# One hand-written line of pieces for all engines, from the start to step 30

## The chip, the cores and the metric

The kernel runs on 1 core of one Trainium2 chip. The metric is device microseconds of that core; lower is better. Before the change: 841.99 us, median of 3 runs (841.66 to 844.39).

## The reference

Three stages in a row, all in fp32 (some weights arrive as 64-bit words and are narrowed by the kernel itself).

```python
# 1. landmark attention: q, k, v are (4, 8, 576, 64); m = 32 landmarks
q_lm = q.reshape(B, H, m, S // m, D).mean(axis=3); k_lm likewise
A  = softmax(scale * q    @ k_lm.T)      # 576 x 32
Bm = softmax(scale * q_lm @ k_lm.T)      # 32 x 32
C  = softmax(scale * q_lm @ k.T)         # 32 x 576
Z  = Bm.T / (norm1(Bm) * norminf(Bm) + 1e-6)
for _ in range(6): Z = 2 * Z - Z @ Bm @ Z
x  = A @ Z @ C @ v                       # then (B*S, H*D) = 2304 x 512
# 2. gated layer: 512 -> 1536 -> 512
x  = (sigmoid(x @ w_gate) * (x @ w_val)) @ w_out
# 3. PReLU layer: 512 -> 2048 -> 512
h  = x @ w_in; out = (relu(h) + alpha * min(h, 0)) @ w_out2
```

## The kernel before

**Stages.** For each of the four batches b the attention makes a small matrix M (`newton`, which runs the six rounds on 32x32 blocks and multiplies with C @ v) and the operand A. M is folded into the gate and value weights of each of six column blocks c (`fold`, L714, and `take`, L736), so that layer 1 is a product of the folded weights We[b, c] with A[b]. Layer 1 and layer 2 of the gated network run in 96 steps, 24 for each b: a step is one half of the tokens (288) times one tile of 128 hidden columns. `layer1` (L763 on) issues 12 matmuls into two PSUM banks (L772), then a sigmoid on ScalarE (L784 for steps before 31, L792 after), a product on VectorE (L785), and `split`, a rounded high part on ScalarE (L136) and the rest on VectorE (L137). `layer2` (L819) issues 12 matmuls two steps later, from `catch_up`. After the 96 steps the PReLU layer runs in 24 pairs (L1140 and L1184) and ends the kernel.

**Weights.** 36 tiles of 64-bit words (24 of w_gate and w_val, 12 of w_out) are loaded by SP (L679, L684) and narrowed: `narrow_scale` (ScalarE, L171), then the low bits either on ScalarE (`narrow_low`, L176) or on VectorE (`narrow_shift`, L182), then two VectorE operations (`narrow_join`, L196 and L198). `convert` does one tile whole: a gate/value tile goes to DRAM for later folds (L702) and, at the fourth tile of a block, `fold` and `take` for b = 0 follow; a w_out tile is split, with the low part on GpSimd, for tiles 1 and 3 on VectorE (`LO_DVE`). Another 32 tiles for the last layer are narrowed by `narrow_w2` or inside `layer1`: two of them at step 30, the others at the steps in `NARROW_AT`.

**First attention.** For b = 0, `first_attention` runs `att_landmarks`, then `newton`, `att_values` and `att_queries` in turns. `transposed` turns six 96-token pieces per pair of heads on TensorE (L251), copies them out on ScalarE (L256) and sums groups of 18 tokens on VectorE (L257). The weights of the softmax for C are turned on TensorE (L392) and copied by ScalarE (L393).

**Later attentions.** `later_attentions` is a generator for b = 1 to 3; each `next` is one piece. The loop over the steps takes 1.75 pieces a step for b = 0 and 2.5 for b = 1 (`ATT_PACE`).

**Order.** Nothing is ordered by hand up to step 30: each engine's order comes out of a scheduler that goes by priority in program order, with `tc.high_priority` for `newton` and some products. From step 31 (`PIN_FROM`) the step's ScalarE, VectorE and load instructions are chained by `pin`. Each engine, and each DMA queue, works its instructions off in that order: one that waits holds up all that stand behind it.

## Time and profile before

| | |
|---|---|
| median of 3 runs | 841.99 us |
| lowest, highest | 841.66, 844.39 us |
| the profiled execution | 845.21 us |
| its span, first to last instruction | 843.4 us |
| TensorE busy | 805.9 us, 96% |
| VectorE busy | 572.0 us, 68% |
| ScalarE busy | 463.7 us, 55% |
| GpSimd busy | 84.4 us, 10% |

Shares over the whole span hide the stages. Rows by stretches of time show what each engine does in a stage; the sigmoids of the steps (L784) serve as marks for where the kernel stands. A view of forms gives the mean duration of each kind of instruction; consecutive instructions of one engine overlap a little, so that such sums come out above the busy time.

### The profile page before, as it was taken

Reading aid. Unit: us, or ns where it says so; the run is one execution under the profiler, and the core shown is the slowest. Engines: PE = TensorE matmul, PEld = TensorE weight load, DVE = VectorE, ACT = ScalarE, POOL = GpSimd, SP = SyncE. Lnnn points to the kernel's source line nnn. Section 1 sums busy time; section 2 is a strip of 40 time slices with the busy share of each in tenths; the row PEclk is TensorE's granted clock in tenths of the full one; section 3 lists DMA queues with packets and bytes.
Section 4 is the critical chain, followed back from the end, with each engine's and each line's share of the span. In section 5 each row is a group of like instructions: output and inputs, shape, how many; then the busy total and the mean of one; then the engine's idle time right before and its main releaser. Section 6 shows DMA issues by size and latency. Waiting matters only on the chain.

```text
span 843.4 us, 15865 instructions
## 1 busy us (share of the span) xinstructions
PE 805.9 (96%) x6033; PEld 710.4 (84%) x6033; DVE 572.0 (68%) x1225; ACT 463.7 (55%) x978; POOL 84.4 (10%) x84
## 2 busy tenths in 40 slices
PE   4779888999999999999999999999999999999996
PEld 4458777787888878999999999898899899899895
DVE  3899988666675564667777887867645568545543
ACT  4768874466664443665555665646543446543443
POOL 0312112121110100252302000000000000000000
PEclk9659999999999999999999999999999999999999
DMA  9779966845345664878366646636633436642002
GB/s 259 274 230 279 290 214 232 230 133 153 113 103 179 227 216 137 267 250 287 129 216 233 208 147 221 217 104 206 191 112 99 144 115 202 221 158 87 1 1 75
DMA packets 75180, 150.99 MB, mean 179 GB/s; under 512 B 9296, under 2 KB 34912, under 8 KB 75104
## 3 DMA queue, kind: packets, MB, share of 16 engines
q1 hardware_dynamic: 71648, 137.40, 50.7%
q0 software_dynamic: 3456, 12.58, 4.7%
q8 instruction: 47, 0.77, 0.4%
q14 instruction: 29, 0.24, 0.1%
...
## 4 chain that ended last, share of the span: by engine, by line
PE 83%; DVE 6%; DMA 4%; issue 3%; ACT 2%; POOL 1%; SPq 1%; POOLq 0%; DVEq 0%; ACTq 0%
PE o L1184 23%; PE prod L1140 21%; PE gv L772 16%; PE acc L819 15%; PE psf L725 3%; PE psq L251 1%; DMA tq<-in_q_dram 1%; PE psc L276 1%; DMA raw<-in_moe_w_val_dram 1%; DMA w2d<-n 1%; DVE wgv L198 1%; DVE wgv L196 1%; POOL wconv L137 0%; PE psd L336 0%; DMA raw<-in_moe_w_out_dram 0%
## 5 line engine op out<-in xcount | busy, mean ns | idle before, releaser
L1140 PE MATMUL prod<-x,w 128*128 128x384 f32 x1008 | 199.7, 337 | 0.0
L1140 PEld LDWEIGHTS prod<-x,w 128*128 128x128 f32 x1008 | 180.3, 188 | 12.8 <-DVE u L1201 0.2
L772 PE MATMUL gv<-A,we 128*128 128x288 f32 x1152 | 189.1, 306 | 1.7 <-ACT g L784 1.0
L772 PEld LDWEIGHTS gv<-A,we 128*128 128x128 f32 x1152 | 163.7, 192 | 21.4 <-issue 17.7
L819 PE MATMUL acc<-gs,wconv 128*128 128x288 f32 x1152 | 180.3, 300 | 1.2 <-DVE part L1033 1.2
L1184 PE MATMUL o<-w,g2s 128*128 128x512 f32 x693 | 180.2, 393 | 0.0
L819 PEld LDWEIGHTS acc<-gs,wconv 128*128 128x128 f32 x1152 | 160.9, 189 | 11.4 <-issue 9.0
L1184 PEld LDWEIGHTS o<-w,g2s 128*128 128x128 f32 x693 | 128.4, 188 | 19.7
L1154 ACT ACTIVATE n<-h 128x384 f32<-128x384 f32 x96 | 50.4, 525 | 87.8 <-DVE h L1201 87.2
L1156 DVE SCALAR_TENSOR_TENSOR h<-n,minus_alpha,h 128x384 f32<-128x384 f32 x96 | 59.2, 617 | 56.4 <-ACT h L1155 55.7
L136 ACT CAST g2s<-h 128x384 fp32r<-128x384 f32 x77 | 39.4, 513 | 49.4 <-DVE h L1156 49.4
L1201 DVE TENSOR_TENSOR h<-u,prod 128x384 f32<-128x384 f32 x72 | 39.8, 553 | 24.3 <-PE prod L1140 20.6
L796 ACT CAST gs<-g 128x288 fp32r<-128x288 f32 x65 | 28.2, 433 | 44.9 <-DVE g L795 44.7
L137 DVE TENSOR_TENSOR g2s<-h,g2s 128x384 fp32r<-128x384 f32 x77 | 42.8, 556 | 13.9 <-ACT g2s L136 11.9
L1155 ACT ACTIVATE h<-h 128x384 f32<-128x384 f32 x96 | 50.4, 525 | 2.7
L795 DVE TENSOR_TENSOR g<-g,gv 128x288 f32<-128x288 f32 x65 | 29.3, 450 | 29.4 <-PE gv L772 25.7
L798 DVE TENSOR_TENSOR gs<-g,gs 128x288 fp32r<-128x288 f32 x65 | 29.7, 457 | 25.9 <-ACT gs L796 25.6
L1184 PE MATMUL o<-w,g2r 128*128 128x512 f32 x171 | 45.2, 393 | 0.0
L171 ACT ACTIVATE raw<-raw 128x512 f32<-128x512 f32 x62 | 40.8, 670 | 8.0 <-DMA raw<-in_moe_w_val_dram 4.0
L792 ACT ACTIVATE g<-gv 128x288 f32<-128x288 f32 x65 | 26.6, 410 | 31.8 <-PE gv L772 31.5
L257 DVE TENSOR_REDUCE lm<-psq 128x32 f32<-128x288 f32 x64 | 27.8, 454 | 17.2 <-ACT kT L256 10.1
L1184 PEld LDWEIGHTS o<-w,g2r 128*128 128x128 f32 x171 | 31.7, 188 | 5.1
...
## 6 DMA issues: line engine op xcount, KB each, us to landing
w<-w7d SPq DMA_DIRECT2D x48, 512.0 KB, 3.4
raw<-in_moe_w_out_dram SPq DMA_DIRECT2D x28, 512.0 KB, 5.2
wgv<-wgvd POOLq DMA_DIRECT2D x24, 512.0 KB, 5.4
w7d<-w SPq DMA_DIRECT2D x24, 512.0 KB, 3.1
raw<-in_moe_w_in_dram SPq DMA_DIRECT2D x16, 512.0 KB, 4.7
...
wgvd<-wgv SPq DMA_DIRECT2D x12, 512.0 KB, 5.1
...
```

The source lines that it names most:

```text
L136: nc.scalar.copy(dst[:, 0, :], src)
L137: (nc.gpsimd if lo == "pool" else nc.vector).tensor_tensor(out=dst[:, 1, :], in0=src, in1=f32(dst[:, 0, :]), op=ALU.subtract)
L171: return nc.scalar.activation(w[:, :, 1], w[:, :, 1], AF.Copy, scale=2.0 ** -112)
L772: nc.tensor.matmul(ps[:, :HB], lhsT=We[b, c, j][:, a, 256 * i + P * s : 256 * i + P * s + P], rhs=att[b, j, "A"][half][:, e, :], start=(n ...
L798: nc.vector.tensor_tensor(out=gs[:, 1, :], in0=g, in1=f32(gs[:, 0, :]), op=ALU.subtract)
L819: nc.tensor.matmul(acc[m][:, :HB], lhsT=wout_sb[f][:, a, P * m : P * m + P], rhs=gs[:, e, :], start=(f == f0 and n == 0), stop=(f == f1 - ...
L1140: nc.tensor.matmul(ps[:, :HG], lhsT=w[:, a, kk], rhs=x7[i, op, kk][:, e], start=(n == 0), stop=(n == 5),)
L1154: nc.scalar.activation(n, h, AF.Relu, scale=-1.0)
L1155: nc.scalar.activation(h, h, AF.Relu)
L1156: nc.vector.scalar_tensor_tensor(out=h, in0=n, scalar=minus_alpha[:, f : f + 1], in1=h, op0=ALU.mult, op1=ALU.add)
L1184: nc.tensor.matmul(acc, lhsT=gs[:, a, P * t : P * t + P], rhs=w2_out[f][:, e, :], start=(count[i, u] == 1 and k == 0), stop=(count[i, u] = ...
L1201: nc.vector.tensor_tensor(out=c, in0=x, in1=ps, op=ALU.add)
```

## The change

The order of TensorE, VectorE, ScalarE, GpSimd and SP up to step 30 is written out as a string of 549 letters, `LINE`, each one piece of work, in a block in which the scheduler keeps the order as written. What was one piece is cut where it passes from one engine to another: `convert` becomes S (ScalarE's part), J (VectorE's) and P (store, or split); `layer1` up to step 30 becomes X (matmuls), Y (sigmoid), y (product), Z (high part), z (low part), and C is `catch_up`; f and t, F and T are the high and low parts of the folds for b = 0 and b = 1. k, q, K, Q, l, L, a, A, v, V and n are the pieces of the first attention, b the pieces of the later ones, p a load of tokens, r a load of a raw weight tile, R a reload of stored weights, s a sigmoid ahead of time to load its table, and h 12 transposes of no use other than to keep TensorE going.

For b = 0 the tokens are loaded in another order, 18 consecutive tokens of one landmark on one partition, so that the landmark sums are additions along a partition (24 VectorE additions in place of 16 reductions), the transposes are 128x128 (36 in place of 48), and the turn of the softmax for C is one VectorE transpose. The rows of the output for b = 0 are stored in that order, in more and smaller transfers. Off VectorE go: the shift for the six even w_out tiles (to ScalarE), the low parts of w_out tiles 1 and 3 (to GpSimd), small scalings and the copies of M for b = 0, and the scaling of C @ v (to ScalarE). Onto VectorE go the low part of A for one half of the heads of b = 0 (from GpSimd), one copy, and the turn just named.

By the end of the line 79 pieces of the later attentions are taken, of 40 for b = 1 and b = 2 each, 39 for b = 3 and two times 8 for the Newton rounds; the rest follows at 4.5 pieces a step from step 31. The two tiles that `narrow_w2` made at step 30 move to steps 33 and 54.

```diff
-    ATT_FROM, ATT_PACE, NEWTON_AHEAD, LO_DVE = 1, (1.75, 2.5), 2000, (1, 3)
+    ATT_FROM, ATT_PACE, NEWTON_AHEAD, LO_DVE = 1, (1.75, 4.5), 2000, ()
...
+    FIRST_DVE, FIRST_POOL = ('q11',), ('0',)
...
+    LINE_NEEDS = {
+        ("l", 0): (("k", 2), ("q", 2)), ("L", 0): (("K", 2), ("Q", 2)),
+        ("L", 1): (("l", 2),),
+        ("a", 0): (("q", 5), ("l", 1)), ("A", 0): (("Q", 5), ("L", 1)),
+        ("v", 0): (("k", 5), ("l", 1)), ("V", 0): (("K", 5), ("L", 1)),
...
+    LINE = (
+        "kkpkqqKrkqkqKKKlqSlavlQQLSpaJrQLLKaSSQvSrLvVlJrSPaaSPJnhVnhVSPJnJJPJrJnvSQPbSnbJ"
+        "nvvnaSJnRSAnpJJSvrnPSvnArSnAbbVPnpvrraPnJSAraAPAPrPVbVbnJASVrAsPPbnbVJSVSJnbhAaf"
+        "SAhStJrPaXRJpYPPyPbXSZPprzYfbyXtYyJbbZXJrzZJPCrJrSbbYCyzrJrPZbXYSyXSJzPZbzfpYySt"
+        "CPpJCXJYSyJfXbZCStpbZzpPYbbrCyZbbXSzbbYPrJbPrpyPbSCbpzZzbSJrbbXpYbySbCPXZbbJCJYp"
+        "PybzZfbtbPXYyrbZzbCXYzCSyZbXJSrYbypPCzbPXYryZbzPSJPCbXYJrSJZPzfpCtyZbzPXYyZbXYby"
+        "zXbbYCpyZzbbrCJbXYZbbrPzyCpbFTZXYyzZzbCbrXYyFRZXYCbTpybbCRzbprXYyFZCZTzXYyzbZXzp"
+        "YyrXYbbryCZbpzFXYTCbZyzbXYybrbpCbZbrXRrzYybbRCZzpXYybbCFTCbCZzZbzCbFT"
+    )
...
-    NARROW_AT = {*range(34, 53, 2), *(58 + 29 * i // 20 for i in range(20))}
+    NARROW_AT = {33, *range(34, 55, 2), *(58 + 29 * i // 20 for i in range(20))}
...
+    def load_first(src, j, nm):
+
+        flat = src[0, 4 * j : 4 * j + 4].rearrange("h (p r) d -> (h p) r d", r=R0)
+        parts = []
+        for r0, r1 in ((0, CUT0), (CUT0, R0)):
+            t = ws_tile(nm, (P, r1 - r0, D), F32)
+            nc.sync.dma_start(out=t, in_=flat[:, r0:r1])
+            parts.append(t)
...
+        (x, y), w = parts, first[j, "work"]
+        add(w[:, :5], x[:, :5], x[:, 5:])
+        yield
+        add(w[:, 5:], y[:, :4], y[:, 4:])
+        add(w[:, :4], w[:, :4], w[:, 5:])
+        add(w[:, :2], w[:, :2], w[:, 2:4])
+        add(w[:, :1], w[:, :1], w[:, 4:5])
+        add(
+            sums[:, a], w[:, 0:1].to_broadcast([P, 2, D]), w[:, 1:2].to_broadcast([P, 2, D])
+        )
...
+        for i in range(3):
+            r = 2 * (3 * n + i)
+            c = r >= CUT0
+            t, r = parts[c], r - CUT0 * c
+            nc.tensor.transpose(
+                ps[:, P * i : P * i + P], t[:, r : r + 2].rearrange("p r d -> p (r d)"), ident
+            )
+        to = first[j, nm][n // 2][:, 3 * (n % 2) : 3 * (n % 2) + 3]
+        (nc.vector.tensor_copy if dve else nc.scalar.copy)(
+            to.rearrange("p i c -> p (i c)"), ps[:, : 3 * P]
+        )
+        if n == 2:
+            del pre[nm, j]
...
+        if b == 0:
+            et = apool.tile([P, R0, LM], F32, tag="et", name="et", bufs=1)
+            nc.vector.transpose(out=et.rearrange("p r l -> p (r l)"), in_=e)
+            att[b, j, "et"] = et
+            return
...
-        nc.vector.tensor_scalar(out=cv, in0=ps[:, :D], scalar1=rd, scalar2=None, op0=ALU.mult)
+        nc.scalar.activation(cv, ps[:, :D], AF.Copy, scale=rd)
...
-            split(a2, at, lo="pool" if b == 0 else "dve")
+            nc.scalar.copy(a2[:, 0], at)
+            yield
+            (nc.gpsimd if b == 0 and str(j) in FIRST_POOL else nc.vector).tensor_tensor(
+                out=a2[:, 1], in0=at, in1=f32(a2[:, 0]), op=ALU.subtract
+            )
...
-                nc.vector.tensor_copy(
+                (nc.scalar.copy if bs[0] == 0 else nc.vector.tensor_copy)(
...
+    def first_loads():
+
+        for j in range(2):
+            for nm, src in (("k", k), ("q", q)):
+                pre[nm, j] = load_first(src, j, "t" + nm)
+        raw_ahead(2)
+        for j in range(2):
+            pre["v", j] = load_first(v, j, "tv")
+        raw_ahead(RAW0 - 2)
...
+    def tile_scale():
+
         kind, c, pr = conv.popleft()
         raw = raws.pop((kind, c, pr))
+        narrow_scale(raw)
         if kind == "o":
+            if c % 2:
+                to = words(raw)[0][:, :, 0]
+            else:
+                to = apool.tile([P, NW], F32, tag="n2", name="n2", bufs=1)
+                narrow_low(raw, to)
+        else:
+            j, u = divmod(pr, 2)
+            if u == 0:
+                wgv[c, j] = ws_tile("wgv", dtype=F32)
+            to = wgv[c, j][:, u]
+            narrow_low(raw, to)
+        scaled.append((kind, c, pr, raw, to))
+
+    def tile_join():
+
+        kind, c, pr, raw, to = scaled.popleft()
+        shifted = kind == "o" and c % 2 == 1
+        if shifted:
+            narrow_shift(raw)
+        narrow_join(raw, to, shifted)
+        joined.append((kind, c, pr, to))
+
+    def tile_done():
+
+        kind, c, pr, to = joined.popleft()
+        if kind == "o":
+            wout_sb[c] = ws_tile("wconv")
+            split(wout_sb[c], to, lo="dve" if c in LO_DVE else "pool")
             return
         j, u = divmod(pr, 2)
         if u == 1:
+            nc.sync.dma_start(out=wgvd[c, j], in_=wgv[c, j])
...
+    def product_one():
+        products.append(step_one(next(begun)))
+    def sigmoid_one():
+        *which, pss = products.popleft()
+        g = bpool.tile([P, HB], F32, tag="g", name="g", bufs=G_BUFS)
+        nc.scalar.activation(g, pss[0][:, :HB], AF.Sigmoid)
+        sigmoids.append((*which, g, pss[1]))
+    def gate_one():
+        *which, g, ps = sigmoids.popleft()
+        nc.vector.tensor_tensor(out=g, in0=g, in1=ps[:, :HB], op=ALU.mult)
+        gates.append((*which, g))
+    def high_one():
+        *which, g = gates.popleft()
+        gs = bpool.tile([P, 2, HB], F32R, tag="gs", name="gs", bufs=GS_BUFS)
+        nc.scalar.copy(gs[:, 0], g)
+        highs.append((*which, g, gs))
+    def low_one():
+        *which, g, gs = highs.popleft()
+        nc.vector.tensor_tensor(out=gs[:, 1], in0=g, in1=f32(gs[:, 0]), op=ALU.subtract)
+        behind.append((*which, gs))
...
+    def keep_busy():
+        ps = bank("idle", "acc")
+        for i in range(12):
+            nc.tensor.transpose(ps[:, P * (i % 4) : P * (i % 4) + P], ident, ident)
...
+    whole = {
+        "X": product_one, "Y": sigmoid_one, "y": gate_one, "Z": high_one, "z": low_one, "C": catch_up, "S": tile_scale,
+        "J": tile_join, "P": tile_done, "r": lambda: raw_ahead(1), "p": load_ahead,
+        "f": lambda: fold_high(0, folded), "t": lambda: fold_low(folded),
+        "F": lambda: fold_high(1, folded_next), "T": lambda: fold_low(folded_next), "h": keep_busy, "b": attend, "s": preload, "R": reload_one, "W": narrow_w2,
+    }
+    done = dict.fromkeys((*streams, *whole), 0)
+    E = mybir.EngineType
+    with tc.manual_schedule(engines={E.PE, E.DVE, E.Activation, E.Pool, E.SP}):
+        for n in LINE:
+            for other, least in LINE_NEEDS.get((n, done[n]), ()):
+                assert done[other] >= least, (n, done[n], other)
+            for other, lead in LINE_LEADS.get(n, ()):
+                assert done[other] >= done[n] + lead, (n, done[n], other)
+            if n in whole:
+                whole[n]()
+            else:
+                next(streams[n], None)
+            done[n] += 1
+    in_line[0] = False
+    for at in range(PIN_FROM, len(steps)):
...
-            if at == NARROW_FROM:
-                with tc.high_priority(NARROW_AHEAD):
-                    narrow_w2()
-                    narrow_w2()
...
-            r, p = divmod(rem, TP)
-            step = min(P - done, TP - p)
+            rr = R if bb else R0
+            half_, rem = divmod(rem, HB)
+            r, p = divmod(rem, S // rr)
+            step = min(P - done, S // rr - p)
             nc.sync.dma_start(
-                out=outv[bb, SIDE[r], p : p + step, :], in_=ob[done : done + step, :]
+                out=outv[rr][bb, 2 * r + half_, p : p + step, :], in_=ob[done : done + step, :]
```

## Rows read from the trace of the kernel before

**Rows 1.** By stage: length; busy PE, PEld, DVE, ACT, POOL; clock, DMA share, GB/s.

```profile
0.00:50.70 50.70, 29.76 (x385) 18.84 (x385) 34.58 (x100) 26.70 (x63) 8.59 (x12) 0.78 0.79 249
50.70:100.90 50.20, 48.37 (x410) 40.90 (x411) 47.48 (x110) 45.26 (x97) 10.31 (x8) 0.91 0.90 285
100.90:142.90 42.00, 35.19 (x386) 28.96 (x385) 36.64 (x95) 27.17 (x60) 9.92 (x10) 0.96 0.69 211
142.90:212.00 69.10, 68.64 (x706) 54.71 (x704) 44.38 (x116) 39.05 (x86) 10.76 (x16) 1.00 0.61 184
212.00:265.00 53.00, 52.25 (x732) 45.38 (x731) 36.53 (x112) 30.75 (x75) 5.80 (x6) 1.00 0.44 129
265.00:460.00 195.00, 195.00 (x1555) 182.97 (x1554) 127.49 (x238) 103.17 (x223) 39.00 (x33) 1.00 0.64 212
```

**Rows 2.** ScalarE in order of time: the sigmoids of steps 0, 10 and 30.

```profile
54.71 0.41 ACT L784 ACTIVATE g<-gv 128x288 f32<-128x288 f32 x1
...
100.88 0.45 ACT L784 ACTIVATE g<-gv 128x288 f32<-128x288 f32 x1
...
211.91 0.41 ACT L784 ACTIVATE g<-gv 128x288 f32<-128x288 f32 x1 [0.42 <-PE gv L772]
```

**Rows 3.** Chain that ended last: one step's layer 1 and layer 2.

```profile
267.31 1.60 PE gv L772 x12
268.91 1.59 PE acc L819 x12
```

**Rows 4.** TensorE's forms from 180 to 260 us, busy us and mean ns.

```profile
L772 PE MATMUL gv<-A,we 128*128 128x288 f32 x177 | 32.1, 311 | 0.0
...
L725 PE MATMUL psf<-wgv,m 64*32 64x512 f32 x48 | 4.7, 601 | 0.0
...
L408 PE MATMUL psv<-vt,et 96*32 96x64 f32 x192 | 4.0, 222 | 0.0
```

**Rows 5.** VectorE's 58 forms up to 212 us: first, last, and those touched.

```profile
L257 DVE TENSOR_REDUCE lm<-psq 128x32 f32<-128x288 f32 x50 | 21.8, 453 | 13.4 <-ACT kT L256 9.1 <-ACT qT L256 4.0
...
L196 DVE TENSOR_SCALAR raw<-raw 128x512 uint16<-128x512 uint16 x13 | 9.7, 759 | 0.1
...
L196 DVE TENSOR_SCALAR wgv<-raw 128x512 uint16<-128x512 uint16 x18 | 9.6, 557 | 0.0
...
L182 DVE TENSOR_SCALAR raw<-raw 128x512 uint32<-128x512 uint32 x13 | 5.4, 429 | 0.0
...
L137 DVE TENSOR_TENSOR wconv<-raw,wconv 128x512 fp32r<-128x512 f32 x2 | 2.5, 1243 | 0.0
...
L990 DVE TENSOR_SCALAR minus_alpha<-alphaT 128x16 f32<-128x16 f32 x1 | 0.2, 174 | 0.0
```

**Rows 6.** ScalarE's 27 forms up to 212 us: first, a table load, last.

```profile
L171 ACT ACTIVATE raw<-raw 128x512 f32<-128x512 f32 x32 | 20.8, 671 | 8.0 <-DMA raw<-in_moe_w_val_dram 4.0 <-DMA raw<-in_moe_w_out_dram 4.0
...
L784 ACT ACT_TABLE_LOAD x6 | 7.7, 1283 | 1.1 <-PE gv L772 1.0
...
L319 ACT ACTIVATION_READ_ACCUMULATOR bm<-psb,bmx 128x1 f32 x2 | 0.4, 193 | 0.0
```

**Rows 7.** GpSimd and VectorE at the same moment, in order of time.

```profile
30.21 1.16 POOL L441 TENSOR_TENSOR ta<-ta,am 128x576 f32<-128x576 f32 x1 [28.90 <-DVE nr L551]
30.23 1.16 DVE L552 TENSOR_SCALAR nr<-nr 128x2 f32<-128x2 f32 x1
```

**Rows 8.** GpSimd's costliest form up to 212 us.

```profile
L137 POOL TENSOR_TENSOR wconv<-raw,wconv 128x512 fp32r<-128x512 f32 x10 | 13.6, 1371 | 62.4 <-ACT wconv L136 55.4 <-DVE we L137 6.9
```

**Rows 9.** ScalarE in order of time: a wait for a weight tile.

```profile
18.38 0.65 ACT L171 ACTIVATE raw<-raw 128x512 f32<-128x512 f32 x1 [3.39 <-DMA raw<-in_moe_w_val_dram]
```

**Rows 10.** DMA from 0 to 60 us, 40 slices of 1.5 us; two issues' sizes.

```profile
GB/s 0 87 312 263 256 261 253 261 260 262 258 371 388 384 403 412 384 397 374 401 410 169 8 0 49 311 342 207 3 0 82 289 344 279 335 277 134 93 284 410
...
raw<-in_moe_w_out_dram SPq DMA_DIRECT2D x6, 512.0 KB, 6.4
...
tk<-in_k_dram SPq DMA_DIRECT2D x4, 288.0 KB, 5.3
```

More of the change, by code (lines that the diff above doesn't have):

```diff
@@ L1 @@
 from collections import deque
+from itertools import count
 from contextlib import ExitStack, nullcontext
@@ L263, in transposed, with first_sums, add @@
         return x
+    def first_sums(nm, j):
+        a, parts = "qk".index(nm), pre[nm, j]
+        if (j, "sums") not in first:
+            first[j, "sums"] = ws_tile("sums", (P, 2, 2, D), F32)
+            first[j, "work"] = ws_tile("work", (P, 9, D), F32)
+            first[j, "lm"] = ws_tile("lm", (P, 2, 4, LM), F32)
+        sums = first[j, "sums"]
+        def add(out, x, y):
+            nc.vector.tensor_tensor(out=out, in0=x, in1=y, op=ALU.add)
+        (x, y), w = parts, first[j, "work"]
[8 more added lines that the diff above has]
+        )
@@ new lines, in first_landmarks, with first_scores @@
+    def first_landmarks(j, ps_tile):
+        sums, lm = first[j, "sums"], first[j, "lm"]
+        ps = ps_tile("psd")[:, : 8 * LM]
+        for a in range(2):
+            nc.tensor.transpose(
+                ps[:, P * a : P * a + P], sums[:, a].rearrange("p e d -> p (e d)"), ident
+            )
+        nc.scalar.copy(lm.rearrange("p a h l -> p (a h l)"), ps)
+    def first_scores(j, ps_tile):
+        ps = ps_tile("psb")[:, :LM]
+        landmark_products(ps, j, first[j, "lm"])
+        landmark_scores(0, j, ps)
@@ new lines, in parts_of, with first_products @@
+    def parts_of(b, j):
+        return att[b, j, "T"] if b else (first.get((j, "q")), first.get((j, "k")), first[j, "lm"])
+    def first_products(pss, heads, lm, xs):
+        for turn_ in range(2):
+            for i, (u, hh, h) in enumerate(heads):
+                e, g = (i + turn_) % 2, 2 * u + hh
+                d = slice(D * e, D * e + D)
+                for x, i0, n in zip(xs, (0, 6), (6, 3)):
+                    nc.tensor.matmul(
+                        pss[e][LM * h : LM * h + LM, LM * i0 : LM * (i0 + n)].rearrange(
+                            "p (i c) -> p i c", i=n
+                        ),
+                        lhsT=lm[d, g],
+                        rhs=x[d, :, LM * g : LM * g + LM],
+                        start=True,
+                        stop=True,
+                    )
@@ L738, in take @@
             We[b, c, j] = ws_tile("we")
[L739 removed]
+            last = split(We[b, c, j], pss[j])
+        return last
     def store_folded(c, pss):
@@ L1044, in tile_landmark_attention_glu_prelu, with step_one @@
         order = [(h, f, f0, f1) for h, f0, f1 in segs for f in range(f0, f1)]
-        for i, (half, f, f0, f1) in enumerate(order):
-            at = 24 * b + i
-            behind.append((b, half, f, f0, f1, layer1(at, b, half, f)))
+        steps.extend((b, *o) for o in order)
+    def step_one(at):
+        b, half, f, f0, f1 = steps[at]
+        return b, half, f, f0, f1, layer1(at, b, half, f)
+    products, sigmoids, gates, highs = deque(), deque(), deque(), deque()
+    folded, folded_next = deque(), deque()
```

373 lines of the change are left out of this document (249 added, 124 removed), and 1 row of the table LINE_NEEDS.

## The prediction

> **What bounds the kernel now.** I read the table by stage first [rows 1], then the sigmoids as marks [rows 2]. From 212 us on TensorE is busy nearly all the time (52.3 of 53.0 us, then 195.0 of 195.0), so work that is moved past that point costs what it takes on TensorE, and the change can only gain before it. There the reader is to see three stages. Up to 50.7 us no engine is full: TensorE 29.8, VectorE 34.6, ScalarE 26.7 us, clock granted at 0.78. From 50.7 to 100.9 us, steps 0 to 10, VectorE is full (47.5 of 50.2) and ScalarE nearly (45.3). From 100.9 to 212 us, steps 10 to 30, TensorE looks busy (35.2 of 42.0, then 68.6 of 69.1).
>
> That last figure hides waits. One step costs TensorE 1.60 + 1.59 = 3.2 us [rows 3]. From 180 to 260 us I see 177 layer-1 matmuls, so 14.75 steps (47 us), three folds (4.7 us) and four attention groups (192 matmuls at 48 a group) [rows 4]; I estimate 4 us for the Newton rounds among them, which leaves (80 - 47 - 4.7 - 4) / 4 = 6.1 us a group. By these prices the work between the sigmoids of steps 10 and 30 is 20 x 3.2 = 64, seven folds at 1.6 = 11, some 2.75 groups = 17 and one Newton run 3: 95 us. It took 211.91 - 100.88 = 111 us. About 16 us are lost there, to waits for VectorE and for loads.
>
> **Positions instead of pieces.** Every engine's order changes at once, so no edit has a price by itself. I add up what each engine must do up to the same mark, take the fullest one, and compare the marks. For the sums each letter of the line got the mean durations of its instructions [rows 5, 6]; instructions overlap, since the 58 forms of VectorE up to 212 us add up to 183 us where the stages show 163 busy [rows 1], so sums count 0.89 for VectorE and, in the same way, 0.91 for ScalarE.
>
> **What VectorE loses and gains.** Off: the shift of six w_out tiles and their in-place join, 6 x (429 + 759 - 557) ns = 3.8 us; two low parts of 1.243 us, 2.5 us [rows 5]; two narrowed tiles, 3.1; scalings and copies, 2.9; and 0.45 of an attention group with the beginnings of a fifth, 5.7, which are only postponed. On: the turn for C, 1.5; a low part and a copy, 1.3; and the landmark sums. These were 16 reductions at 453 ns, 7.3 us [rows 5]. The 24 additions have no row; by VectorE's small and large operations they lie between 5 and 11 us, and I take 8.5. Net 14 us of rows, 12 busy: 163 becomes about 151 (149 to 154). Adding up the letters gives 154, of which 49 before the first X, 49 from there to the eleventh, 55 to the end. ScalarE comes to about 143, against 138: 46, 50 and 47. TensorE has 47 us in the second part (ten steps, five folds, 1.45 groups) and 88 in the third (20 steps 64, seven folds 11, 1.65 groups 10, Newton 3). GpSimd stays near 30. The 48 idle transposes and the turns of b = 0 stand ahead of the first X, where TensorE has 24 us of work in 60: covered. The small scalings that ScalarE takes over have no row; I took the 193 ns of its last form [rows 6] for ten of them, 2 us (1 to 4), in its sum.
>
> ScalarE's figure holds the unseen term. A table load takes 1.283 us [rows 6], and the scores of the later groups stand between sigmoids; I count eight loads in the second part, 10 us, estimated from the order of the letters. The bounds are 4 loads and 16: 5 us less, 10 more.
>
> **Where the Trainium skill speaks against it.** GpSimd's operation at 30.21 us takes 1.16 us, and a VectorE operation on 128x2 elements beside it takes the same 1.16 us [rows 7], where the last form of the VectorE view, on 128x16, takes 174 ns [rows 5]. The Trainium skill, "SBUF - State Buffer", section "Who interferes with whom", says that these two engines share one pair of ports under an exclusive lock; the row agrees. By that rule the two low parts moved to GpSimd (1.371 us each [rows 8]) could hold VectorE up for as long as they take and return nothing of the 2.5 us above. The Trainium skill, "ScalarE: Activation LUTs", section "Rules for kernel authors", wants all functions of one table set done before a switch and sets 2.7 us for it; the row of 1.283 us decides here, and by the page the second part would be 11 us longer on ScalarE.
>
> **The first sigmoid.** Before, ScalarE stood 3.39 us at a weight tile queued ahead of the landmarks [rows 9], while loads ran at about 260 GB/s for tokens and 390 for weights, with slices of nothing where SP waited [rows 10]. After the change the fifth S is the 40th letter; it needs 3.5 MB of tokens and five weight tiles of 512 KB: 13.6 + 6.7 us and 2.4 to start, so 23 us, and is done at 24.4. From there to the first X ScalarE has 36.9 us of rows, 33.6 busy, and a table load: 59.3. VectorE, from the first tokens at 5.5 us, has 49: 54.5 at the earliest. So the first sigmoid falls at about 61.5 us, and not at 54.7 [rows 2]: the change narrows 17 tiles ahead of it where the old order had narrowed six or so. This costs 7 us and is the price for a lighter second part. Should ScalarE not wait for tiles, it could be 58; should both engines wait for each other as before, 66.
>
> **The later marks.** The second part is even: 49 VectorE, 50 ScalarE, 47 TensorE, and 15 MB of transfers that fit (at 300 GB/s, 50 us at worst, and weights ran at 390). SP issues them in the order of the line: a token load whose buffer is not free holds up the weight tiles behind it and so S, and a store of narrowed weights waits for J. At the 94% that VectorE reached there before [rows 1] it takes 53: step 10 at 114.7 us, 14 behind the old 100.9. In the third part VectorE has 55 and ScalarE 47 beside TensorE's 88; TensorE is the bound, as it was from 180 to 260 us with the same load, and the price per group already holds the waits of that stretch. Step 30 comes at 202.7 us against 211.9. From the 9.2 us, the postponed 0.55 group goes off, 0.55 x 6.1 = 3.3. It is done from step 31 to 43, where VectorE is at 69% [rows 1]: TensorE's price is all of it. The two postponed tiles cost VectorE 2 us there and nobody else. The more numerous output stores for b = 0 are issued on SP amid the last layer, where TensorE has work enough; if not covered they would be a few transfers of under half a us. The gain is 5.9 us. The profiled execution, 845.2 us with a span of 843.4, becomes 839; it lies 0.4% above the median, and against the median of 841.99 the time becomes 836.
>
> **Rivals.** *A denser line* (gain 10 to 16 us). The second part runs full from 58 us: step 10 at 108, step 30 at 196, minus 3.3: 12.6 gained, 829; with waits of 180 to 260 us gone too, some 4 more, 825. For it: in a fixed order nothing unwanted can come ahead, as the tile did [rows 9]. Against it: three engines would have to be full at once.
> *No change worth measuring* (840 to 844): less than 2.5 us, 0.3%, is about what a measurement of this kernel can tell from nothing. It comes about if the line does not what it says, that is if the second part keeps its waits and only trades steps against tiles.
> *Slower, by waits in the second part.* The place is the stretch between the first and the eleventh X, where all three engines carry about 50 us and each piece of ScalarE or VectorE holds the next of the other up, with the order fixed: a late piece cannot be passed by. At a fill of 75% it takes 67 us, step 10 comes at 128 and step 30 at 216; with 3.3 for the rest, 7.6 us lost: 850. It decides at a fill of 85%: step 10 at 120.6 leaves nothing. VectorE had 95% in one stage and 87% in the next [rows 1], which is for the forecast, but it was then the one full engine, which is for this.
>
> **How the numbers follow.** Forecast, gain 3 to 11 us (831 to 839): 0.48, and its time is 836. Denser, 825 to 831: 0.16. No change: 0.15. Slower: 0.21. The first two are faster: 0.64; same 0.15; slower 0.21. The range for eight in ten runs from 821 (the denser case, with five table loads fewer) to 848, short of the full price of the slow case.
>
> **What would show it.** Right: the first sigmoid near 61 us, the eleventh near 115, the 31st near 203; VectorE's busy time up to there near 151; TensorE without gaps after the eleventh; a granted clock of 1.00 from the first X (the 0.91 of the old second stage [rows 1] would cost 9% of 47 us, some 4). Wrong: an eleventh sigmoid after 121, more than twelve table loads between the first and the eleventh, SP or GpSimd standing at a load while weights are wanted, or a stage past step 31 that is longer by more than 4 us.

## The result, and the profile after

The changed kernel takes 835.03 us (median of 4 runs, 834.33 to 835.8) beside 841.83 for the kernel before: a ratio of 0.9913, 95% interval 0.989 to 0.9935. A second set beside the last experiments gave 836.3 and 842.97, ratio 0.9929 (0.9907 to 0.9951). So it is 6.8 us faster (6.7 in the second set), against a forecast of 5.9 and a time of 836. The profiled executions are further apart, 845.21 and 834.3 us, since that of before lies 3.4 us above its median. Marks are compared below, and differences of one us between marks of two kernels are not read: up to step 10 the same order gave marks up to 1.5 us apart from run to run.

| sigmoid of step | 0 | 10 | 30 | 31 | 45 | end of span |
|---|---|---|---|---|---|---|
| before, us | 54.7 | 100.9 | 211.9 | 217.0 | 282.2 | 843.4 |
| forecast | 61.5 | 114.7 | 202.7 | | | |
| after | 61.1 | 107.6 | 185.2 | 199.9 | 270.5 | 832.6 |

Between the marks, before and after: 46.2 and 46.5 (steps 0 to 10), 111.0 and 77.6 (10 to 30), 5.1 and 14.7 (30 to 31), 65.2 and 70.6 (31 to 45), 561.2 and 562.1 (the rest). The gain of 33.4 us is all in the third part; 6.4 us are lost ahead of the first sigmoid, and 16 are given back right behind step 30.

ScalarE after, in order of time, the sigmoids that [rows 2] shows of before:

```profile
61.09 0.43 ACT L1342 ACTIVATE g<-gv 128x288 f32<-128x288 f32 x1
...
107.63 0.41 ACT L1342 ACTIVATE g<-gv 128x288 f32<-128x288 f32 x1
...
185.15 0.41 ACT L1342 ACTIVATE g<-gv 128x288 f32<-128x288 f32 x1 [0.58 <-DVE gs L1358]
```

By stage, columns as in [rows 1], cut at the marks; first after, then before from step 10 on:

```profile
0.00:61.10 61.10, 42.60 (x703) 34.93 (x703) 48.91 (x131) 44.62 (x102) 14.55 (x19) 0.75 0.96 331
61.10:107.60 46.50, 45.08 (x476) 37.74 (x478) 42.67 (x106) 39.59 (x88) 9.72 (x7) 1.00 0.81 260
107.60:185.20 77.60, 77.32 (x824) 67.60 (x813) 53.72 (x139) 40.73 (x99) 12.90 (x15) 1.00 0.50 154
185.20:199.90 14.70, 13.86 (x139) 10.66 (x137) 8.65 (x22) 7.81 (x16) 2.20 (x3) 1.00 0.62 189
199.90:270.50 70.60, 68.64 (x905) 59.52 (x905) 48.37 (x138) 47.03 (x107) 8.47 (x10) 1.00 0.48 146
```

```profile
100.90:211.90 111.00, 103.74 (x1087) 83.58 (x1086) 80.92 (x210) 66.12 (x144) 20.68 (x25) 0.98 0.64 194
...
217.00:282.20 65.20, 64.45 (x827) 56.70 (x826) 41.67 (x121) 35.49 (x83) 6.86 (x8) 1.00 0.44 133
```

Two things are to be seen. After the first sigmoid TensorE has no more gap worth naming (45.1 of 46.5, then 77.3 of 77.6), so from 61 us on the kernel is as long as TensorE's work. And the third part got shorter by more than its gaps: before, TensorE was busy for 103.7 us there and idle for 7. The rest is work that now lies elsewhere, and work that takes less time. TensorE's forms in the third part, before and then after:

```profile
L819 PE MATMUL acc<-gs,wconv 128*128 128x288 f32 x240 | 42.5, 311 | 1.2 <-DVE part L1033 1.2
L772 PE MATMUL gv<-A,we 128*128 128x288 f32 x238 | 42.2, 310 | 0.0
L725 PE MATMUL psf<-wgv,m 64*32 64x512 f32 x128 | 11.3, 601 | 0.0
```

```profile
L1061 PE MATMUL gv<-A,we 128*128 128x288 f32 x238 | 36.1, 301 | 0.0
L1104 PE MATMUL acc<-gs,wconv 128*128 128x288 f32 x192 | 29.5, 303 | 0.0
L1015 PE MATMUL psf<-wgv,m 64*32 64x512 f32 x96 | 7.1, 601 | 0.0
```

Layer 1 has the same 238 matmuls in both and keeps TensorE busy for 6.1 us less (why is not shown: the mean of one is 301 ns beside 310). Layer 2 has 48 matmuls fewer, so four steps, and the folds 32 fewer, so two. TensorE's sequence right behind step 30 shows where the layer-2 steps went:

```profile
185.95 1.83 PE L1104 MATMUL acc<-gs,wconv 128*128 128x288 f32 x12
187.72 1.09 PE L1015 MATMUL psf<-wgv,m 64*32 64x512 f32 x16
...
195.09 1.09 PE L1015 MATMUL psf<-wgv,m 64*32 64x512 f32 x16
196.11 1.84 PE L1061 MATMUL gv<-A,we 128*128 128x288 f32 x12
```

Four layer-2 steps and two folds come before the next layer 1, that of step 31 at 196.11. The line's last letters are the work that had been left over.

### The profile page after: what moved, and what is told of

It reads as the page before. It is cut to its first block, busy times and chain, and to the rows that moved or that the text cites. A ratio compares the mean times of both kernels' runs of the same rounds, so it can differ in the third digit from the quotient of the medians.

```text
span 832.6 us, 16450 instructions
## 1 busy us (share of the span) xinstructions
PE 802.2 (96%) x6313; PEld 715.7 (86%) x6313; DVE 567.2 (68%) x1213; ACT 467.4 (56%) x994; POOL 85.3 (10%) x85
## 4 chain that ended last, share of the span: by engine, by line
PE 89%; DMA 5%; DVE 3%; ACT 1%; issue 1%; SPq 1%; POOL 0%; DVEq 0%; ACTq 0%; POOLq 0%
PE o L1541 24%; PE prod L1497 21%; PE gv L1061 18%; PE acc L1104 18%; PE psf L1015 3%; DMA raw<-in_moe_w_val_dram 2%; PE psq L313 1%; DMA raw<-in_moe_w_out_dram 1%; DMA rawA<-in_moe_w_val_dram 1%; PE psc L424 1%; PE psz L726 1%; PE psd L496 0%; SPq L296 0%; PE psa L424 0%; PE psv L592 0%
## 5 line engine op out<-in xcount | busy, mean ns | idle before, releaser
L1497 PE MATMUL prod<-x,w 128*128 128x384 f32 x1008 | 199.9, 337 | 0.6 <-ACT p L1565 0.6
L1061 PE MATMUL gv<-A,we 128*128 128x288 f32 x1152 | 177.6, 300 | 1.3 <-ACT g L1077 0.8
L1061 PEld LDWEIGHTS gv<-A,we 128*128 128x128 f32 x1152 | 157.9, 188 | 21.5 <-issue 16.1
L1104 PE MATMUL acc<-gs,wconv 128*128 128x288 f32 x1152 | 175.0, 299 | 0.0
L1104 PEld LDWEIGHTS acc<-gs,wconv 128*128 128x128 f32 x1152 | 158.6, 188 | 6.6 <-issue 5.7
L1513 DVE SCALAR_TENSOR_TENSOR h<-n,minus_alpha,h 128x384 f32<-128x384 f32 x96 | 59.2, 617 | 54.4 <-ACT h L1512 53.7
L1558 DVE TENSOR_TENSOR h<-u,prod 128x384 f32<-128x384 f32 x72 | 39.8, 553 | 24.4 <-PE prod L1497 20.7
L1558 DVE TENSOR_TENSOR h<-p,prod 128x384 f32<-128x384 f32 x24 | 13.3, 553 | 27.4 <-PE prod L1497 27.4
```

Source lines behind the costliest of these rows:

```text
L1061: nc.tensor.matmul(ps[:, :HB], lhsT=We[b, c, j][:, a, 256 * i + P * s : 256 * i + P * s + P], rhs=att[b, j, "A"][half][:, e, :], start=(n ...
L1104: nc.tensor.matmul(acc[m][:, :HB], lhsT=wout_sb[f][:, a, P * m : P * m + P], rhs=gs[:, e, :], start=(f == f0 and n == 0), stop=(f == f1 - ...
L1497: nc.tensor.matmul(ps[:, :HG], lhsT=w[:, a, kk], rhs=x7[i, op, kk][:, e], start=(n == 0), stop=(n == 5),)
L1513: nc.vector.scalar_tensor_tensor(out=h, in0=n, scalar=minus_alpha[:, f : f + 1], in1=h, op0=ALU.mult, op1=ALU.add)
L1558: nc.vector.tensor_tensor(out=c, in0=x, in1=ps, op=ALU.add)
```

## The experiments

**The same pieces in the scheduler's order.**

```diff
-    with tc.manual_schedule(engines={E.PE, E.DVE, E.Activation, E.Pool, E.SP}):
+    with nullcontext():
```

> The changed kernel with the same pieces in the same program order, but without the block that keeps the order: the scheduler orders every engine. Theory A, the fixed order gains (TensorE without gaps between the sigmoids of steps 10 and 30, 78 us): without it that stretch goes back to 95 us or more and the kernel to 845 to 860 us. Rival B, less VectorE work and the new token layout gain, whatever the order: 833 to 838 us, the stretch at 78 to 84 us.

872.04 us, ratio 1.0352 (1.0315 to 1.0388): 30 us slower than the kernel before, and worse than the theory that the order is what counts had put it. The first sigmoid comes at 72.7, steps 10 to 30 take 92 us. The pieces without the written order are a loss.

**The edits in the old order.** The kernel before with the low parts of w_out tiles 1 and 3 on GpSimd, the low bits of the even tiles on ScalarE and the scaling of C @ v on ScalarE:

```diff
-    ATT_FROM, ATT_PACE, NEWTON_AHEAD, LO_DVE = 1, (1.75, 2.5), 2000, (1, 3)
+    ATT_FROM, ATT_PACE, NEWTON_AHEAD, LO_DVE = 1, (1.75, 2.5), 2000, ()
...
-        nc.vector.tensor_scalar(out=cv, in0=ps[:, :D], scalar1=rd, scalar2=None, op0=ALU.mult)
+        nc.scalar.activation(cv, ps[:, :D], AF.Copy, scale=rd)
...
-            to = words(raw)[0][:, :, 0]
-            narrow(raw, to)
+            if c % 2:
+                to = words(raw)[0][:, :, 0]
+                narrow(raw, to)
+            else:
+                to = apool.tile([P, NW], F32, tag="n2", name="n2", bufs=1)
+                narrow(raw, to, act=True)
```

> The kernel before with three of the edits alone: the low parts of w_out tiles 1 and 3 on GpSimd, the low bits of the six even w_out tiles on ScalarE, the scaling of C @ v on ScalarE; some 8 us less VectorE work in rows before step 30. Rival B: 835 to 838 us, most of the gain. Theory A: 839 to 843 us, since VectorE is full only from 50 to 100 us and TensorE's order stays.

848.39 us, ratio 1.0076 (1.005 to 1.0102). One theory expected most of the gain, the other about the old time, and both miss: with less VectorE work the kernel became 6.8 us slower. Steps 0 to 10 take 49.1 us (46.2 before), steps 10 to 30 112.6. The next run answers for 2.3 us of this; the rest stays open.

**Of these, the two low parts alone.**

```diff
-    ATT_FROM, ATT_PACE, NEWTON_AHEAD, LO_DVE = 1, (1.75, 2.5), 2000, (1, 3)
+    ATT_FROM, ATT_PACE, NEWTON_AHEAD, LO_DVE = 1, (1.75, 2.5), 2000, ()
```

> The kernel before with one of the three edits that came out slower together (848.4 against 841.8): only the low parts of the w_out tiles 1 and 3 go to GpSimd, the order is the scheduler's. Theory A (GpSimd needs longer for a low part and the gv of those steps waits for it, or its subtraction holds VectorE up): 843 to 847, and steps 0 to 10 take over 47 us. Theory B (the loss is that of the narrowing on ScalarE and of the scalings there): within 1 us of 841.8, steps 0 to 10 in 46 us.

845.44 us, ratio 1.0027 (1.0016 to 1.0038); 2.3 us slower. Steps 0 to 10 take 50.2 us, 4.0 more; steps 10 to 30 take 107.1, 3.9 less, but beside an execution of before that lies 3.4 us above its median, so the marks do not settle where the 2.3 us are lost. What the move does to VectorE stands in the order of time, GpSimd's two low parts and the VectorE instructions beside them:

```profile
52.86 2.91 POOL L137 TENSOR_TENSOR wconv<-raw,wconv 128x512 fp32r<-128x512 f32 x2 [6.93 <-ACT wconv L136]
```

```profile
53.30 1.48 DVE L196 TENSOR_SCALAR raw<-raw 128x512 uint16<-128x512 uint16 x1
54.57 1.51 DVE L196 TENSOR_SCALAR wgv<-raw 128x512 uint16<-128x512 uint16 x1
```

These two forms have means of 759 and 557 ns in [rows 5]; beside GpSimd they took 1480 and 1510. VectorE's narrowing forms up to 212 us, this kernel first, then the changed one:

```profile
L196 DVE TENSOR_SCALAR raw<-raw 128x512 uint16<-128x512 uint16 x13 | 12.8, 1015 | 0.7 <-ACT raw L171 0.7
L196 DVE TENSOR_SCALAR wgv<-raw 128x512 uint16<-128x512 uint16 x18 | 10.7, 619 | 0.0
```

```profile
L233 DVE TENSOR_SCALAR wgv<-raw 128x512 uint16<-128x512 uint16 x18 | 8.3, 459 | 0.0
L233 DVE TENSOR_SCALAR raw<-raw 128x512 uint16<-128x512 uint16 x6 | 4.6, 759 | 0.4
```

In the old order the two forms cost (1015 - 759) x 13 + (619 - 557) x 18 = 4.4 us more than before, and six tiles of a third form 1.0 us less: 3.4 us, against 2.5 of subtractions taken off (over all narrowing forms VectorE has 61.5 us instead of 55.5). In the line the two forms run at 459 and 759 ns, not above those of before. That this stretching is what made the kernel slower fits, and is not shown by itself.

**The same undone in the changed kernel**, the two low parts back on VectorE:

```diff
-    ATT_FROM, ATT_PACE, NEWTON_AHEAD, LO_DVE = 1, (1.75, 4.5), 2000, ()
+    ATT_FROM, ATT_PACE, NEWTON_AHEAD, LO_DVE = 1, (1.75, 4.5), 2000, (1, 3)
```

> The changed kernel with one edit undone: the low parts of the w_out tiles 1 and 3 are subtracted on VectorE again, not on GpSimd. Theory A (VectorE's work ahead of step 30 is what sets the marks, and a moved instruction returns its length): two subtractions of about 1.2 us come back on VectorE in the stretch to the eleventh sigmoid, of which VectorE is full, so the time is 1 to 2.5 us above the changed kernel's 835.0, that is 836 to 837.5. Theory B (the GpSimd subtraction holds VectorE up for as long as it saved, or the two fall into idle time): within 0.8 us of it.

837.43 us, ratio 0.9938 (0.9925 to 0.995), 1.1 and 2.4 us above the two medians of the changed kernel. The first sigmoid is at 63.5, where seven runs of the same order up to it (the changed kernel twice, and five that differ later or by the idle transposes alone) have 61.1 to 62.6. The later mark speaks for a small return by the move. By the times alone the two kernels are not told apart, since the intervals overlap.

**By hand up to step 10 only.** The first 311 letters, up to just ahead of the eleventh X, keep their order; the rest of the line is given in the same order, but to the scheduler.

```diff
-        for n in LINE:
+        for n in LINE[:311]:
...
+    with nullcontext():
+        for n in LINE[311:]:
```

> The changed kernel with the order kept by hand only up to the eleventh sigmoid (the first 311 letters); the other 238 pieces are given in the same order, but to the scheduler, which orders the engines. Theory A (the 33 us that the third part gained come from the order inside it): the eleventh sigmoid stays at 107.6 within 1.5, steps 10 to 30 take 90 to 95 us instead of 77.5 (92 with the whole line given to the scheduler), and the time is 847 to 853. Theory B (they come from the state in which the line leaves the kernel at step 10: tiles narrowed, tokens there, attention of the next group done): steps 10 to 30 take 77 to 81, and the time is 834 to 839.

850.41 us, ratio 1.009 (1.0076 to 1.0104); steps 10 to 30 take 91.7 us. So 14 us of the third part's gain come from the order inside it; the other 19 are there without it. But TensorE was busy there from end to end. The fold matmuls of this kernel from 107.6 to 185.2 us:

```profile
L1015 PE MATMUL psf<-wgv,m 64*32 64x512 f32 x96 | 16.8, 601 | 0.0
```

The same six folds keep TensorE for 16.8 us instead of the 7.1 shown with the result. In order of time, one fold in this kernel, and below it one in the changed kernel:

```profile
112.82 1.05 PE L1015 MATMUL psf<-wgv,m 64*32 64x512 f32 x4
113.80 0.30 PE L592 MATMUL psv<-tv,et 96*32 96x64 f32 x2
114.03 1.04 PE L1015 MATMUL psf<-wgv,m 64*32 64x512 f32 x2
```

```profile
107.95 1.61 PE L1015 MATMUL psf<-wgv,m 64*32 64x512 f32 x16
```

Two matmuls of a fold take as long as four (1.04 and 1.05 us), and sixteen in one piece 1.61: they run side by side while nothing of another shape stands between them. The Trainium skill, "TensorEngine Tiling (Array Packing)", section "Key Properties", says that tiles work in parallel and that a change of the tiling drains the engine; the rows agree in that each block begins anew at over 1 us. The kernel before ties the matmuls of a fold for b = 0 to one VectorE instruction (`behind_of`, L733), so that they become ready together; the changed kernel has no such tie. So this run, and the first one, lack the tie as well as the order; the pieces in the scheduler's order with the tie were not run, but the next run has the folds in one piece. In the first one the fold matmuls up to 460 us took 10 of the 30 us more than in the kernel before, which stands first:

```profile
L725 PE MATMUL psf<-wgv,m 64*32 64x512 f32 x384 | 31.6, 620 | 0.5 <-DVE m L594 0.2 <-DVE wgv L198 0.2
```

```profile
L1015 PE MATMUL psf<-wgv,m 64*32 64x512 f32 x384 | 41.9, 611 | 3.6 <-DMA wgv<-wgvd 3.6
```

**TensorE alone by hand, from step 10 on.** As the run before, with TensorE's order restored:

```diff
-    with nullcontext():
+    with tc.manual_schedule(engines={E.PE}):
         for n in LINE[311:]:
```

> As the run that kept all engines by hand only up to the eleventh sigmoid, but with TensorE alone kept by hand in the rest of the line too (VectorE, ScalarE, GpSimd and the DMA queue are ordered by the scheduler there). In that run the third part took 91.7 us, TensorE busy throughout, with the same 96 fold matmuls at 16.8 us busy instead of 7.1: the scheduler had put other small matmuls between them. Theory A (what the order is worth in the third part is TensorE's own sequence, above all folds in one piece): steps 10 to 30 take 77 to 81 us, the fold matmuls 7 to 8 us, and the time is 834 to 839. Theory B (the other engines' sequence matters as much, because their pieces hold each other up): 85 to 91 us, and the time is 843 to 850.

845.18 us, ratio 1.0028 (1.0016 to 1.004); steps 10 to 30 take 87.4 us. The folds are in one piece again (8.0 us for the 96), yet only 4.3 of the 14 us come back. TensorE's two longest waits from 108.8 to 196.2 us (the changed kernel has none over 0.3 us from 107.6 to 185.2):

```profile
PE pse L560 <- ACT e L531: 2.9, 1, 2.9
PE psf L1015 <- ACT e L531: 1.2, 1, 1.2
```

With TensorE's sequence fixed and ScalarE's not, an exponential that ScalarE has put off holds up everything behind it, folds included (5.4 us idle). TensorE is also busy for longer, 82.0 us instead of 77.3; 1.9 of that is one layer-2 step more ahead of the mark (204 matmuls for 192). The theory that TensorE's sequence is what counts (77 to 81 us) falls; the other one (85 to 91) holds.

**TensorE alone by hand, whole line.**

```diff
-    with tc.manual_schedule(engines={E.PE, E.DVE, E.Activation, E.Pool, E.SP}):
+    with tc.manual_schedule(engines={E.PE}):
```

> The changed kernel with TensorE alone kept by hand in the whole line; the other engines and the DMA queue are ordered by the scheduler. With everything given to the scheduler it took 872 us, with the first sigmoid at 72.7, steps 0 to 10 in 53.4 and steps 10 to 30 in 92. Theory A (TensorE's sequence is what counts from the first sigmoid on, the other engines' and the queue's order before it): the first sigmoid at 68 to 74, steps 0 to 10 in 46 to 50, steps 10 to 30 in 77 to 82, the time 842 to 852. Theory B (where VectorE and ScalarE are full, their order counts too): steps 0 to 10 take 53 us or more, the time 852 to 870.

862.29 us, ratio 1.0252 (1.021 to 1.0295): the first sigmoid at 74.7, steps 0 to 10 in 53.5, steps 10 to 30 in 87.2. The marks are those of the profiled execution, which is the slowest of four (868.16). Again the second theory: before step 10, too, a fixed TensorE gains nothing while VectorE and ScalarE are ordered otherwise.

**Fewer tiles ahead of the first X.** The prediction put the later first sigmoid down to the tiles narrowed ahead of it. Here the letters S, J, P and r past the eighth tile move behind the first X, which becomes the 139th letter instead of the 170th (the J that ends the line's first row goes as well):

```diff
...
-        "nvvnaSJnRSAnpJJSvrnPSvnArSnAbbVPnpvrraPnJSAraAPAPrPVbVbnJASVrAsPPbnbVJSVSJnbhAaf"
-        "SAhStJrPaXRJpYPPyPbXSZPprzYfbyXtYyJbbZXJrzZJPCrJrSbbYCyzrJrPZbXYSyXSJzPZbzfpYySt"
+        "nvvnanRAnpvrnPvnArnAbbVPnpvraPnAaAAVbVbnAVAsbnbVVnbhAafAhtaXJSJpSYJJSySSbrXJSZrPp"
+        "PrzPYJfSbryPXPtJYSySJbSbSZJXrPRzJZPPPCSPrJJbrbJYPCryJzrSrJrZPbXYSyXSJzPZbzfpYySt"
...
```

> The changed kernel with the line's narrowing beyond the eighth tile moved from ahead of the first X to behind it, the rest in the same order. If narrowing 17 tiles first is what makes the first sigmoid late, it comes at 48 to 54 us instead of 61.1. If VectorE and ScalarE set the eleventh sigmoid all the same, that stays at 105 to 110 us and the kernel at 834 to 837 us; if the first X is what counts, the kernel goes to 826 to 829 us.

851.87 us, ratio 1.0122 (1.0085 to 1.0158). The first sigmoid comes at 61.5, and the sixth at 97.6 instead of 80.6; the eleventh comes at 124.7, which neither theory had. Stages from 50 us on, the changed kernel first, then this one:

```profile
50.00:61.50 11.50, 10.89 (x132) 8.53 (x138) 7.58 (x15) 8.69 (x22) 3.77 (x4) 0.73 0.82 309
61.50:80.60 19.10, 18.88 (x218) 14.95 (x203) 18.06 (x45) 16.39 (x37) 4.46 (x3) 1.00 0.91 291
```

```profile
50.00:61.50 11.50, 10.42 (x120) 8.11 (x121) 3.58 (x7) 5.64 (x15) 1.40 (x1) 0.70 0.17 63
61.50:80.60 19.10, 13.63 (x110) 10.28 (x108) 17.18 (x37) 13.96 (x28) 5.03 (x5) 0.82 0.60 200
```

VectorE now has 3.6 us of work in the 11.5 us ahead of the first sigmoid, and loads run at 63 GB/s. The tiles had filled time in which the way to the first sigmoid left VectorE free, and behind it they come late: TensorE, in its fixed order, is busy for 13.6 of the next 19.1 us instead of 18.9. In the changed kernel the chain of waits to the first sigmoid passes over the load of a weight tile, then over C @ v, M and the first fold:

```profile
34.01 7.27 DMA rawA<-in_moe_w_val_dram
...
51.21 1.48 PE psv L579 x48
...
56.80 1.07 PE psf L1015 x16
```

In this run the same stretch of it, from C @ v on, is held up by something else: TensorE has no work from 48.07 us until a token load of the next batch lands, 11.9 us after its issue.

```profile
50.45 0.69 PE L307 MATMUL psq<-ident,tq 96*128 96x96 f32 x6 [2.39 <-DMA tq<-in_q_dram]
```

So the run shows that narrowing fewer tiles first does not bring the sigmoid to 48 to 54 us; the 2.4 us of this wait may hide a smaller gain.

**Without the idle transposes.** The letter h is left out of the line.

```diff
-        "kkpkqqKrkqkqKKKlqSlavlQQLSpaJrQLLKaSSQvSrLvVlJrSPaaSPJnhVnhVSPJnJJPJrJnvSQPbSnbJ"
+        "kkpkqqKrkqkqKKKlqSlavlQQLSpaJrQLLKaSSQvSrLvVlJrSPaaSPJnVnVSPJnJJPJrJnvSQPbSnbJ"
-        "nvvnaSJnRSAnpJJSvrnPSvnArSnAbbVPnpvrraPnJSAraAPAPrPVbVbnJASVrAsPPbnbVJSVSJnbhAaf"
+        "nvvnaSJnRSAnpJJSvrnPSvnArSnAbbVPnpvrraPnJSAraAPAPrPVbVbnJASVrAsPPbnbVJSVSJnbAaf"
-        "SAhStJrPaXRJpYPPyPbXSZPprzYfbyXtYyJbbZXJrzZJPCrJrSbbYCyzrJrPZbXYSyXSJzPZbzfpYySt"
+        "SAStJrPaXRJpYPPyPbXSZPprzYfbyXtYyJbbZXJrzZJPCrJrSbbYCyzrJrPZbXYSyXSJzPZbzfpYySt"
```

> The changed kernel without the 48 transposes of no use. If they keep the clock up: the granted clock in the first 59 us falls under 0.74 and the steps after it are slower, 836 to 839 us. If they only stand in TensorE's way (one dozen lies on the chain at 54.7 us, 2.1 us): first sigmoid at 59 instead of 61.1, 833 to 834 us.

836.57 us, ratio 0.9927 (0.9902 to 0.9952): not told apart from the changed kernel, and the first sigmoid at 61.7 and steps 0 to 10 in 46.5 us meet neither theory. The granted clock is 0.53 instead of 0.67 from 20 to 40 us, 0.67 instead of 0.50 from 40 to 50, and 1.00 from the first sigmoid on in both: the idle transposes shift the slow stretch, and no mark shows anything else.

**Less left for later.** Nine more attention pieces at the line's end:

```diff
-        "YyrXYbbryCZbpzFXYTCbZyzbXYybrbpCbZbrXRrzYybbRCZzpXYybbCFTCbCZzZbzCbFT"
+        "YyrXYbbryCZbpzFXYTCbZyzbXYybrbpCbZbrXRrzYybbRCZzpXYybbCFTCbCZzZbzCbFTbbbbbbbbb"
```

> The changed kernel with nine more attention pieces at the end of the line, so that less attention work is left for the stretch after step 31. Theory A (work that is postponed costs its TensorE time wherever it stands, since TensorE has no gap from the eleventh sigmoid on): the sigmoid of step 30 stays, that of step 31 comes 4 to 6 us later, that of step 45 stays within 1 us of 270.5, and the time is within 1 us of 835.0. Theory B (postponed work costs more than its TensorE time, because behind step 31 VectorE and ScalarE have the steps' own work and the next group's scalings in front of it): step 45 comes 2 to 4 us earlier, and the time is 831 to 833.

833.86 us, ratio 0.9897 (0.9882 to 0.9912): the lowest time of all, 1.2 and 2.4 us below the two medians of the changed kernel, with intervals that overlap: faster than it by the medians, not beyond doubt. The sigmoid of step 31 did not come 4 to 6 us later but 1.4, the one of step 40 5.7 later, that of step 45 at 269.6; the stretch from 31 to 45 takes 68.3 us instead of 70.6 (70.8 in the second set). That lies between the two theories.

**TensorE in program order after step 31 as well.** As the run before, and:

```diff
     for at in range(PIN_FROM, len(steps)):
+        with tc.manual_schedule(engines={E.PE}) if at < 44 else nullcontext():
```

> The changed kernel with nine more attention pieces at the line's end, and TensorE kept in the order of the program (steps, layer 2 two steps behind, attention pieces between them) for steps 31 to 43 as well. There the scheduler had the attention matmuls apart: the stretch from the sigmoid of step 31 to that of 45 took 70.6 us in the changed kernel and 68.3 with the nine pieces alone. Theory A (TensorE's sequence is worth there what it is worth in the third part): 64 to 67 us for the stretch, and a time of 829 to 832.5. Theory B (attention pieces in program order make TensorE wait for VectorE and ScalarE, which a scheduler would fill with later steps): 70 us or more, and a time of 836 or more.

836.28 us, ratio 0.9925 (0.9901 to 0.9949); the stretch from 31 to 45 takes 71.0 us, and layer 1 waits 1.8 us for sigmoids and 0.9 for products. By these numbers it gives back what the nine pieces had gained: the second theory, as in the two runs with TensorE alone by hand.

**The changed kernel again.**

> The changed kernel once more, beside these runs on the same chip, for comparison: ratio to the kernel before between 0.989 and 0.9935, the first sigmoid within 1 us of 61.1, steps 10 to 30 in 77 to 78 us. Both theories expect the same here.

836.3 us, ratio 0.9929; first sigmoid at 61.9, steps 10 to 30 in 77.5 us.

## Why the prediction was right, and where it wasn't

The time, the sign and the outline of the mechanism held: a gain before step 30, part of it given back behind it. The size came out right by luck, because three errors nearly cancel: the second part was 6.5 us shorter than put, the third 10.4, and the work put off cost 12.6 more. Two of them are in good part one error seen twice: layer-2 steps and folds of some 8 us, by the prediction's prices, were counted ahead of step 30 and stand behind it. With the first sigmoid this leaves a gain of 10.6; the two profiled executions are 10.9 apart, 4.1 of which is that they lie on opposite sides of their medians, by 3.4 and 0.7.

*The first sigmoid* was forecast at 61.5 and came at 61.1, but not on the path of the sum. The sum has ScalarE at work without a stop from the fifth tile on, 34.9 us from 24.4; the fifth tile was done at 22.4, and ScalarE was busy for 30.9 of the 38.7 us from there. VectorE's 49 us were met (48.9). The reason given, "the change narrows 17 tiles ahead of it", was not borne out: with those past the eighth behind it, the sigmoid came at 61.5, held by a token load. The chain of waits of the changed kernel goes over a weight tile's load that lands at 41.3, C @ v, M and the first fold. What would bring the mark forward stays open.

*The second part* was put at 53 us and took 46.5. VectorE's share was mis-sized, 49 against 42.7: the letters were counted up to the wrong X, 19 too far. The step that failed is that VectorE sets this part: its fill of 92%, beside the 94% used, agrees, but the fullest engine is TensorE, 45.1 of 46.5 us. Its 47 us (by the prediction's own prices ten steps, five folds and 1.45 groups are 48.9) were overcounted: the rows have 108 / 12 = nine layer-2 steps, 48 / 16 = three folds and 80 / 48 = 1.67 groups, 16 + 14.3 + 4.8 + 10.2 = 45.3. ScalarE's term for table loads was too large too: four in this part, not eight, so the lower bound of 4 to 16 was the value. From 61.1 to 107.6 us, TensorE and ScalarE:

```profile
L1104 PE MATMUL acc<-gs,wconv 128*128 128x288 f32 x108 | 16.3, 302 | 0.0
L1015 PE MATMUL psf<-wgv,m 64*32 64x512 f32 x48 | 3.4, 600 | 0.0
L592 PE MATMUL psv<-tv,et 96*32 96x64 f32 x80 | 1.5, 221 | 0.0
```

```profile
L474 ACT ACT_TABLE_LOAD x2 | 2.6, 1283 | 0.0
L1342 ACT ACT_TABLE_LOAD x2 | 2.6, 1283 | 0.0
```

*The third part* was put at 88 us and took 77.6. The content was overcounted: 20 layer-2 steps, seven folds and 1.65 groups, where the rows show 192 / 12 = 16 layer-2 steps, 96 / 16 = six folds and, with 80 matmuls of C @ v, 80 / 48 = 1.67 groups. With the prediction's own prices this is 32 + 25.4 + 9.6 + 10.2 + 3 = 80.2; the folds at their measured 7.1 make it 77.7. That TensorE is the bound there, without gaps, was right. The 16 us "lost there, to waits" in the old order were not all waits: TensorE was idle for 7.3 us, eight folds and three groups stood there where seven and 2.75 were counted (98 us by the prices and not 95), and the same matmuls of layer 1 took 6.1 us more than after.

*The work put off* was the term that failed most: 3.3 us for 0.55 of a group. From step 30 to 45 the kernel after needs 15.0 us more than before and 0.9 more to the end. The line reaches the sigmoid of step 30 with its layer 2 behind: up to step 45 there are 216 layer-2 matmuls instead of 180, so 36 / 12 x 1.59 = 4.8 us; 48 fold matmuls instead of 16, two folds of 1.1 to 1.6; and 144 matmuls of C @ v instead of 96, a whole group, 6.1. That is 13.1 to 14.1 of the 15. I had counted the attention pieces left and not the other streams. The sign that was named for a wrong step, a stage past step 31 that is longer by more than 4 us, shows: 70.6 against 65.2, and 9.6 more between steps 30 and 31. From 185.2 to 270.5 us after, and from 211.9 to 282.2 before:

```profile
L1104 PE MATMUL acc<-gs,wconv 128*128 128x288 f32 x216 | 36.5, 306 | 0.0
L1015 PE MATMUL psf<-wgv,m 64*32 64x512 f32 x48 | 3.3, 601 | 0.0
L592 PE MATMUL psv<-tv,et 96*32 96x64 f32 x144 | 3.0, 222 | 0.4 <-ACT et L561 0.4
```

```profile
L819 PE MATMUL acc<-gs,wconv 128*128 128x288 f32 x180 | 28.6, 301 | 0.0
L408 PE MATMUL psv<-vt,et 96*32 96x64 f32 x96 | 2.0, 222 | 0.0
L725 PE MATMUL psf<-wgv,m 64*32 64x512 f32 x16 | 1.1, 601 | 0.0
```

*VectorE's work* up to step 30 is 48.9 + 42.7 + 53.7 = 145.3 us, below the 149 to 154. The 24 additions come to 8.6 us for an estimate of 8.5. Missed, in part, was the stretching: before, 24 narrowing operations took 557 and 618 ns where the changed kernel has 459 and 456 (18 x 98 + 6 x 162 = 2.7 us). GpSimd "stays near 30" was a wrong reading: up to step 30 it had 39.6 us before [rows 1] and has 37.2 after; nothing hung on it.

*The lock.* That the moved low parts "return nothing of the 2.5 us above" is right for the old order, where moving the two low parts cost 2.3 us, and is not seen in the line, where undoing the move made the kernel 1.1 and 2.4 us slower, with intervals that overlap. The Trainium skill, "SBUF - State Buffer", section "Who interferes with whom", names which VectorE operations contend with a GpSimd operation that reads SBUF: those with two SBUF inputs, and copies and tensor_scalar in their fast forms, but not reductions. The rows agree: beside GpSimd a narrowing `TENSOR_SCALAR` took 1480 ns, and two reductions (453 ns the mean in [rows 5]) 0.79 us. I had weighed it as one price for all. In the line one of the two low parts stands beside a transpose and two reductions, which ran at their usual length:

```profile
50.45 1.29 POOL L173 TENSOR_TENSOR wconv<-raw,wconv 128x512 fp32r<-128x512 f32 x1 [1.11 <-ACT wconv L171]
```

```profile
50.29 0.77 DVE L660 STREAM_TRANSPOSE at<-ta 128x576 f32<-128x576 f32 x1
50.99 0.79 DVE L321 TENSOR_REDUCE lm<-psq 128x32 f32<-128x288 f32 x2
```

*The rivals.* Of the denser line the marks at step 10 came true (108 against 107.6), and the one at step 30 was passed (196 against 185.2); its total did not, because of the work put off. The slower case did not come about here, but its mechanism is real: with the tiles moved behind the first X, steps 0 to 5 took 36 us instead of 19.5, because in a fixed order a late tile can't be passed by.

*Left open*: how much of the 14 us that the order inside the third part is worth belongs to each of VectorE, ScalarE, GpSimd and the DMA queue. The folds have 8 to 10 of TensorE's time, but with TensorE's order alone restored only 4.3 came back. What the new token layout is worth by itself was not run.
